# Weights loaded by casting transfers, chunk loads in 1 KB runs with the token group first, in a fused attention and feed-forward kernel

## The chip, the cores and the metric

The kernel runs on one core of a Trainium2 chip. The metric is device microseconds of one execution. Each kernel was run several times. The engines are called by their profile names: PE is the tensor engine (PEld its weight loads), DVE the vector engine, ACT the scalar engine, POOL GpSimd, and SP the engine that issues most of the transfers. Each works through its own instruction queue in the order in which the build put the instructions.

## The reference

Sliding-window causal attention (window 64) over 8 batches, 8 heads, 576 positions and head size 64 gives 4608 tokens of width 512. A feed-forward layer with squared ReLU follows.

```python
scores = q @ k.T / sqrt(64), masked to 0 <= row - column < 64, softmax
x = (softmax @ v), heads side by side          # [4608, 512]
h = np.maximum(x @ w_in, 0.0)                  # w_in  [512, 2048]
out = (h * h @ w_out).astype(np.float32)       # w_out [2048, 512]
```

Everything arrives and leaves in fp32. The kernel multiplies in fp16.

## The kernel before

The 4608 tokens are 36 chunks of 128. A chunk covers two blocks of 64 tokens, and its first block also looks at the 64 tokens before it. Four functions do a chunk's attention: T (transpose k and q on PE, evict kT on DVE and qT on ACT), S (scores on PE, exponential on ACT, mask on DVE), V (values on PE, division on DVE), and X (transpose of the result). Then come up groups (x times w_in, ReLU on ACT, square on DVE) and output matmuls (times w_out).

For V, the values lie in two forms. `v_ev` holds a chunk's own 128 tokens. `v_od` holds the 64 tokens before the chunk and its first 64. So a chunk's `v_od` is written in two halves, and the lower half comes from the chunk **before** it. The eight buffers of each form rotate:

```python
NV = 8
v_evs = [const.tile([P, H, 66], FP16, name=f"v_ev{i}") for i in range(NV)]
v_ods = [const.tile([P, H, 66], FP16, name=f"v_od{i}") for i in range(NV)]
...
nc.vector.memset(v_ods[0][0:64, :, 0:D], 0.0)

def load(i):
    ...   # three fp32 transfers on SP: k, q, v; the source is read in runs of 64 values, 256 B
    nc.gpsimd.tensor_copy(out=k16s[i][:], in_=...)          # casts to fp16 on POOL
    nc.gpsimd.tensor_copy(out=q16s[i][:], in_=...)
    v_ev, v_od, v_next = v_evs[i % NV], v_ods[i % NV], v_ods[(i + 1) % NV]
    nc.gpsimd.tensor_copy(out=v_ev[:, :, 0:D], in_=sts[2][:])
    nc.gpsimd.tensor_copy(out=v_od[64:P, :, 0:D], in_=v_ev[0:64, :, 0:D])
    if i + 1 < NCK:
        nc.gpsimd.tensor_copy(out=v_next[0:64, :, 0:D], in_=v_ev[64:P, :, 0:D])

def values(i):
    ...
    for blk in range(2):
        vv = (v_ods if blk == 0 else v_evs)[i % NV]
        nc.tensor.matmul(av[...], pms[i][...], vv[:, h, 0:65], start=True, stop=True)
```

Chunk 0 has no tokens before it. The mask sets these probabilities to zero, so what the lower half of `v_ods[0]` holds does not matter to its result, as long as it is finite.

The first eight chunks (the first stage, `NFIRST = 8`) have no earlier group to work on, so they are handled chunk by chunk with small up groups (four blocks of 128 columns at a time). After them, every group g does its up groups beside the output matmuls of group g-1 and the attention of group g+1. This is the order in which the program text of before states the first stage; `warm(n)` are filler matmuls without use to the result:

```python
load(0)
for s in load_w_in():          # 16 fp32 transfers of 256 KB, each cast (times 100) by DVE
    s()
for i in range(1, NV - 1):     # chunks 1 to 6
    load(i)
T(0), warm(6), S_(0), warm(6), V(0), warm(6), X(0), warm(4)
load(NV - 1)                   # chunk 7, AFTER V(0)
for s in load_w_out() + ffn_up_chunk(0):   # 16 more transfers, cast by POOL
    s()
T(1), S_(1), warm(2), V(1), T(2), warm(2), X(1), S_(2)
for i in range(1, NFIRST):
    up = ffn_up_chunk(i)
    up[0](), V(i + 1), T(i + 2), up[1](), up[2](), X(i + 1), S_(i + 2), up[3]()
```

And a scheduler in the build then sorts each engine's queue, by priorities and by when it thinks each instruction can start; only engines named in a "manual schedule" region keep the text's order, and what stands outside the region can still be put in between (e5 shows it).

The softmax here doesn't subtract the row's maximum and nothing guards it: scores larger than these inputs give would overflow.

## Time and profile before

| | before |
|---|---|
| time, median of 3 runs (lowest to highest) | 347.73 us (346.21 to 348.35) |
| span of the profiled execution | 345.9 us |
| PE busy over the span | 94% |
| first value matmul of chunk 0 starts at | 15.2 us |
| last matmul of the small up groups starts at | 75 us |

The busy time by window, before. Each row gives the window, its length, the busy microseconds (and instruction counts) of PE, PEld, DVE, ACT and POOL, the granted PE clock, the DMA share (packet times summed, over 16 engines; the sum can pass 1), and GB/s.

```profile
core 0: us, PE busy (x) PEld busy (x) DVE busy (x) ACT busy (x) POOL busy (x), PEclk, DMA share, GB/s
...
16.00:24.00 8.00, 5.99 (x82) 4.41 (x81) 5.49 (x15) 1.79 (x3) 0.61 (x1) 1.00 0.90 255
24.00:32.00 8.00, 4.52 (x64) 3.41 (x64) 5.46 (x14) 2.32 (x5) 5.57 (x9) 0.65 1.07 243
32.00:40.00 8.00, 7.04 (x130) 6.17 (x129) 5.76 (x14) 4.70 (x10) 6.64 (x12) 0.92 0.96 216
40.00:50.00 10.00, 8.49 (x164) 7.49 (x162) 8.56 (x19) 5.66 (x11) 9.44 (x17) 1.00 0.99 256
...
140.00:200.00 60.00, 60.00 (x532) 29.91 (x531) 40.98 (x95) 30.55 (x55) 30.57 (x50) 1.00 0.70 168
```

At 140 to 200 us PE is busy for all 60 of 60 us: nothing but less PE work could shorten that part. What a change in loads can move lies in the first 75 us, where PE has gaps, and the rows from 16 to 50 us show it working, with gaps, while transfers run at full load.

The chain of waits, before, in its first 25 us; columns are start, duration, and what.

```profile
4.12 5.49 DMA ws<-in_moe_w_in_dram
...
10.09 4.25 DMA ws<-in_moe_w_in_dram
...
14.81 3.77 DMA ws<-in_moe_w_in_dram
...
19.72 5.40 DMA ws<-in_moe_w_in_dram
```

These four transfers take 18.9 of the first 25 us, so w_in is what bounds the start.

First PE, before: start, duration, line, instruction, and in brackets how long the engine had been idle and what released it.

```profile
13.65 1.25 PE L286 MATMUL warm<-mask_inner,ident 128*128 128x512 f16 x5
15.17 0.22 PE L211 MATMUL av<-v_od_121,pm_327 128*64 128x65 f16 x1 [0.26 <-DVE pm_327 L201]
```

The first value matmul of chunk 0 starts at 15.17 us and has waited 0.26 us, for its mask. It reads `v_od_121`, which is `v_ods[0]`. Then POOL, before:

```profile
47.83 0.61 POOL L167 COPY v_od_121<-v_ev_120 64x512 f16<-64x512 f16 x1
```

At 47.83 us, chunk 7's last copy writes the same `v_od_121`, for chunk 8. It comes 33 us after the matmul, and the matmul does not wait for it, since `load(7)` stands after V(0) in the program.

### The profile page before, as it was taken

How to read it: one execution, taken by the hardware profiler on the slowest of the kernel's cores; microseconds unless marked ns; L12 is line 12 of the kernel's file. 1: busy time of each engine (PE TensorE's matmuls, PEld its weight loads, DVE VectorE, ACT ScalarE, POOL GpSimd, SP SyncE). 2: the span in 40 equal slices, each digit the busy share in tenths (PEclk: the TensorE clock that was granted, in tenths of full speed). 3: DMA queues.
4: the chain of work that ended last, by engine and by line, in shares of the span. 5: the costliest groups of instructions: out<-in, count | busy, mean ns of one | idle time of the engine just before them, and what ended most of it. 6: DMA issues, size and time to landing. Idle time of an engine off the chain costs nothing.

```text
span 345.9 us, 7917 instructions
## 1 busy us (share of the span) xinstructions
PE 324.3 (94%) x3146; PEld 178.2 (52%) x3146; DVE 207.9 (60%) x506; ACT 163.8 (47%) x289; POOL 121.5 (35%) x204
## 2 busy tenths in 40 slices
PE   1957888999999999999999999999999999999995
PEld 0346787875555555445545554455445544544442
DVE  2656988852666776676776657665675566544400
ACT  1123457544535646643664466436544654444411
POOL 4009895497753333316566544530000000000000
PEclk9996999999999999999999999999999999999998
DMA  7799987899972455546877757730011000000021
GB/s 200 249 252 239 234 247 252 207 230 228 243 172 61 93 121 123 121 124 155 212 185 182 170 135 184 185 87 27 23 45 36 30 32 32 30 30 32 35 88 62
DMA packets 122341, 46.65 MB, mean 135 GB/s; under 512 B 113600, under 2 KB 113600, under 8 KB 122304
## 3 DMA queue, kind: packets, MB, share of 16 engines
q1 hardware_dynamic: 122304, 46.15, 51.7%
q8 instruction: 24, 0.39, 0.5%
q14 instruction: 13, 0.11, 0.1%
HBM read 36.70 MB, written 9.44 MB: 133 GB/s over the span
## 4 chain that ended last, share of the span: by engine, by line
PE 83%; DVE 7%; DMA 5%; ACT 2%; SPq 1%; issue 1%; ACTq 0%
PE ops L296 37%; PE hps L250 28%; DMA ws<-in_moe_w_in_dram 5%; PE qkT_ps L173 4%; PE av L211 4%; PE xt_ps L224 2%; DVE h_397 L276 1%; DVE h_1087 L276 1%; DVE xT L226 1%; DVE w_in_sb L117 1%; PE hps_639 L271 1%; SPq L151 1%; SPq L115 0%; PE hps_1088 L271 0%; PE hps_1537 L271 0%
## 5 line engine op out<-in xcount | busy, mean ns | idle before, releaser
L250 PE MATMUL hps<-xT,w_in_sb 128*128 128x512 f16 x448 | 115.2, 379 | 0.0
L254 ACT ACTIVATE hrelu<-hps 128x512 f32<-128x512 f32 x112 | 66.8, 598 | 91.6 <-PE hps L250 90.9
L250 PEld LDWEIGHTS <-w_in_sb 128*128 128x128 f16 x448 | 43.7, 98 | 52.6 <-issue 0.3
L271 PEld LDWEIGHTS <-w_in_sb 128*128 128x128 f16 x512 | 31.2, 99 | 8.2 <-issue 3.9
L301 ACT ACTIVATE osb<-ops 128x512 f32<-128x512 f32 x36 | 21.6, 600 | 29.1 <-PE ops L296 28.9
L182 ACT ACTIVATE qT<-qkT_ps 128x512 f16<-128x512 f16 x36 | 21.5, 596 | 22.6 <-DVE kT L180 22.3
L216 DVE TENSOR_TENSOR x_sb<-av,rden 128x256 f16<-128x256 f32 x72 | 27.5, 415 | 0.1
L180 DVE COPY kT<-qkT_ps 128x512 f16<-128x512 f16 x36 | 15.2, 421 | 18.0 <-PE qkT_ps L173 17.8
L226 DVE COPY xT<-xt_ps 128x512 f16<-128x512 f16 x36 | 15.1, 420 | 12.7 <-PE xt_ps L224 12.7
L215 DVE RECIPROCAL rden<-av 128x4 f32<-128x4 f32 x72 | 11.4, 178 | 17.1 <-PE av L211 17.1
L255 DVE SCALAR_TENSOR_TENSOR h_5222<-hps,hrelu 128x512 f16<-128x512 f32 x16 | 11.1, 691 | 16.6 <-ACT hrelu L254 16.6
L296 PE MATMUL ops<-w_out_sb,h_1087 128*128 128x512 f16 x64 | 17.5, 380 | 0.0
L191 PEld LDWEIGHTS <-kT 64*128 64x128 f16 x576 | 11.0, 95 | 12.2 <-issue 9.6
L296 PE MATMUL ops<-w_out_sb,h_3120 128*128 128x512 f16 x64 | 16.5, 380 | 0.0
L296 PE MATMUL ops<-w_out_sb,h_2579 128*128 128x512 f16 x64 | 16.5, 380 | 0.0
L296 PE MATMUL ops<-w_out_sb,h_4199 128*128 128x512 f16 x64 | 16.5, 380 | 0.0
L296 PE MATMUL ops<-w_out_sb,h_3658 128*128 128x512 f16 x64 | 16.5, 380 | 0.0
L296 PE MATMUL ops<-w_out_sb,h_2041 128*128 128x512 f16 x64 | 16.5, 380 | 0.0
L296 PE MATMUL ops<-w_out_sb,h_4736 128*128 128x512 f16 x64 | 16.4, 379 | 0.0
L296 PE MATMUL ops<-w_out_sb,h_397 128*128 128x512 f16 x64 | 15.3, 380 | 0.0
L224 PE MATMUL xt_ps<-ident,x_sb 128*128 128x128 f16 x144 | 15.1, 222 | 0.1
L255 DVE SCALAR_TENSOR_TENSOR h_4736<-hps,hrelu 128x512 f16<-128x512 f32 x16 | 11.0, 689 | 6.8 <-ACT hrelu L254 6.4
(837 smaller groups left out, 611.1 us busy)
## 6 DMA issues: line engine op xcount, KB each, us to landing
out_dram<-osb SPq DMA_DIRECT2D x36, 256.0 KB, 2.2
k_st<-in_k_dram SPq DMA_DIRECT2D x32, 256.0 KB, 3.9
q_st<-in_q_dram SPq DMA_DIRECT2D x32, 256.0 KB, 4.0
v_st<-in_v_dram SPq DMA_DIRECT2D x32, 256.0 KB, 4.1
ws<-in_moe_w_in_dram SPq DMA_DIRECT2D x16, 256.0 KB, 4.2
k_st<-in_k_dram SPq DMA_DIRECT2D x8, 128.0 KB, 3.2
q_st<-in_q_dram SPq DMA_DIRECT2D x8, 128.0 KB, 3.0
v_st<-in_v_dram SPq DMA_DIRECT2D x8, 128.0 KB, 3.2
```

Source lines behind the costliest of these rows:

```text
L173: nc.tensor.transpose(out=ps[:, s, hp, :], in_=src[i][:, hp * P:(hp + 1) * P], identity=ident[:])
L180: nc.vector.tensor_copy(out=kT[:, :, 64:192], in_=ps[:, 0])
L182: nc.scalar.activation(out=qT[:], in_=ps[:, 1], func=AF.Copy, scale=1.0)
L216: nc.vector.tensor_tensor(out=x_sb[:, 4 * half:4 * half + 4, :], in0=av[:, :, 0:D], in1=rden[:].to_broadcast([P, 4, D]), op=ALU.mult)
L224: nc.tensor.transpose(out=xt[:, c, :], in_=xs[i][:, 2 * c:2 * c + 2, :], identity=ident[:])
L226: nc.vector.tensor_copy(out=xT_of(i // 4)[:, :, (i % 4) * P:(i % 4 + 1) * P], in_=xt[:])
L250: nc.tensor.matmul(hps[:], w_in_sb[:, c, f * P:(f + 1) * P], xT_of(g)[:, c, :], start=(c == 0), stop=(c == DMC - 1))
L254: nc.scalar.activation(out=hrelu[:], in_=hps[:], func=AF.Relu)
L255: nc.vector.scalar_tensor_tensor(out=h2s[g][:, f, :], in0=hps[:], scalar=0.0, in1=hrelu[:], op0=ALU.max, op1=ALU.mult)
L271: nc.tensor.matmul(hps[:, f, :], w_in_sb[:, c, (4 * fq + f) * P:(4 * fq + f + 1) * P], xT_of(g)[:, c, t0:t0 + P], start=(c == 0), stop=(c ...
L296: nc.tensor.matmul(hold["ps"][:], h2s[g][:, f, ts * P:(ts + 1) * P], w_out_sb[:, f, :], start=(f == 0), stop=(f == FFC - 1))
L301: nc.scalar.activation(out=osb[:], in_=hold["ps"][:], func=AF.Copy, scale=OUT_SCALE)
```

## The change

The intent is to take work off DVE and POOL and bytes and descriptors off the transfers, so that the first stage is shorter:

- w_in and w_out come in by eight transfers issued from POOL that cast fp32 to fp16 on the way. The 32 casts on DVE and POOL go. The scale of 100 that the w_in cast carried becomes a scale of 1e4 in the ReLU. That POOL has to issue them agrees with the Trainium skill, "DMA: Bandwidth & Descriptors", section "SWDGE vs HWDGE vs iDMA", which names GpSimd as the only engine whose transfers may cast.
- k and q of the seven first-stage chunks that lie within one batch are read in runs of 1 KB (four tokens of one head) in two transfers each. A partition then holds token group and head pair instead of a token. The token group (32 of them) is the slower dimension and the head pair (4) the faster. The rows are put right when kT and qT are evicted from PSUM, with strided reads.
- ACT casts k and q of the first stage (chunk 0's k on DVE), not POOL.
- POOL's and PE's queues in the first stage are fixed by manual-schedule regions. For this the loads of all eight chunks are written in one POOL block, ahead of the attention.

The core of the diff (cut):

```diff
-            nc.sync.dma_start(out=ws[:], in_=moe_w_in[c * P:(c + 1) * P, quar * FQ:(quar + 1) * FQ])
-            nc.vector.tensor_scalar(out=w_in_sb[:, c, ...], in0=ws[:], scalar1=W_SCALE, ...)
+        nc.gpsimd.dma_start(                     # fp32 in DRAM, fp16 in the tile
+            out=w_in_q[quar][:],
+            in_=moe_w_in[:, quar * FQ:(quar + 1) * FQ].rearrange("(c p) n -> p c n", p=P))
 ...
+                for b2 in range(2):
+                    eng.dma_start(
+                        out=st[:, b2, :],
+                        in_=rows.rearrange("(a b) (t r) d -> b t a (r d)", b=2, r=4)[b2])
 ...
+        if runs(i):
+            k_dst, q_dst = [x.rearrange("p a (i r) -> p a i r", r=4) for x in (k_dst, q_dst)]
+            k_src, q_src = [x.rearrange("p r (i a) -> p a i r", a=HP) for x in (k_src, q_src)]
+        nc.vector.tensor_copy(out=k_dst, in_=k_src)
 ...
-    load(0)
-    for s in load_w_in():
-        s()
-    for i in range(1, NV - 1):
-        load(i)
-    T(0), warm(6), S_(0), warm(6), V(0), warm(6), X(0), warm(4)
-    load(NV - 1)
-    for s in load_w_out() + ffn_up_chunk(0):
-        s()
+    with tc.manual_schedule(engines={mybir.EngineType.Pool}):
+        load(0)
+        load_w_in(0)
+        load_w_in(1)
+        cast_v(0)
+        load_w_in(2)
+        load(1)
+        load_w_in(3)
+        for i in range(2, NV):
+            load(i)
+            if i >= 6:
+                load_w_out(2 * i - 12)
+                load_w_out(2 * i - 11)
+    with tc.manual_schedule(engines={mybir.EngineType.PE}):
+        T, S_, V, X = transposes, scores, values, to_xT
+        U = up_chunk
+        T(0), warm(3), S_(0), warm(3), V(0), warm(3), X(0), warm(2)
+        U(0, 0), warm(2), U(0, 1), T(1), warm(2), S_(1), warm(2), V(1), U(0, 2), X(1), U(1, 0)
+        ...
```

## The prediction

It was made from the text, the profile of before, and the instruction order of the built changed kernel, before that kernel had run.

> **What bounds it now.** The span is 345.9 us, TensorE busy 94% (busy table). Busy time by window splits it: from about 75 to 342 us TensorE never rests (60.0 of 60 us at 140 to 200, clock 1.00), 267 us of work that the change leaves, then 4 us of drain. Only the first 75 us can move. There the chain of waits runs through w_in transfers until 25 us (5.5, 4.3, 3.8, 5.4 us), then through eight small chunk stages of about 7 us each, where DVE is busy 87 to 90% and DMA moves 210 to 255 GB/s. TensorE work in that stage is small: 32 up groups of about 0.9 us, and about 1.3 us of attention a chunk, near 39 us.
>
> **What changes by intent.** Sixteen DVE casts of w_in (0.43 us) and sixteen POOL casts of w_out (0.61 us) go; the DMA casts instead. The k and q casts of chunks 0 to 7 go to ACT (about 0.6 us each). Seven chunks' k and q load in 1 KB runs, not 256 B. Token-group-first keeps 32, not 4, as the slowest dimension on the DRAM side; the Trainium skill, "DMA: Bandwidth & Descriptors", section "Why a DMA increments its semaphore by 16 and not by 1", says that this dimension decides over how many of the 16 engines a DMA spreads. No trace here shows it yet. Strided PSUM reads may lift kT's eviction from 0.42 to about 0.6 us, hidden. Alone, all this would end the stage 10 us sooner.
>
> **What the built instruction order does** should cost more:
> 1. ACT's queue holds the k and q casts of all chunks up to 7 ahead of the first hrelu. It is in order, so no up group is squared before chunk 7's q has landed.
> 2. PE's queue holds output matmuls of group 0 among the first chunks: one that waits for the first quarter of w_out stands before chunk 1's values, the second quarter follows, the third and fourth stand before chunk 3's scores. POOL issues the first two quarters only after chunk 6's v is cast.
>
> So PE stops after chunk 1's scores until about 4.2 MB of w_in, 5.5 MB of chunks 0 to 6, 2.1 MB of w_out and part of chunk 7 have landed: 12 to 12.6 MB. At 250 to 280 GB/s (estimate from the rates above) plus 3 us of start and latency this is about 48 us (42 to 56).
>
> **Sum.** After the restart 30 up groups, most of seven chunks' attention and about 31 early output matmuls (0.22 us each) remain: 42 us of TensorE, about 47 with dependences, a colder clock and the last w_out quarters. The stage ends at about 95 us. The early matmuls take 7 us from the later 267: 95 + 260 + 4 = 359 us. Prediction: **359 us**, 8 in 10 between 347 and 373. Chances: faster by over 2% 0.06, within 2% 0.23, slower by over 2% 0.71.
>
> **What would show it.** PE almost idle from about 14 to 45 us, a lowered clock after it; the first hrelu at 35 us or later, behind ACT's casts that wait for DMA; PE's output matmuls waiting for w_out transfers; DMA over 0.8 busy until 55 us; afterwards the same full PE; kT's eviction near 0.6 us.
>
> **What would make it wrong.** DMA well above 300 GB/s would restart PE near 40 us and make it a tie. Slow casting transfers, or many us of descriptor generation on POOL (in no trace yet), would make it slower still. If PE and ACT were not held by those early instructions, with all w_in landed by 25 us, the result would be near 335 us.

## More of the kernel before

A reader of a buffer waits for the writers that stand before it in the text.

From the page of before, the lines to compare later: the kT eviction (busy us in all, mean ns of one), and the queue that carried the loads.

```profile
L180 DVE COPY kT<-qkT_ps 128x512 f16<-128x512 f16 x36 | 15.2, 421 | 18.0 <-PE qkT_ps L173 17.8
...
q1 hardware_dynamic: 122304, 46.15, 51.7%
```

## The result, and the profile after

| | before | after |
|---|---|---|
| time, median of 4 runs (lowest to highest) | 348.04 us (346.21 to 348.37) | 369.42 us (367.33 to 369.64) |
| ratio of fast runs (95% interval) | | 1.0613 (1.0572 to 1.0654) |
| profiled span | 345.9 us | 367.9 us |
| first value matmul of chunk 0 starts at | 15.2 us | 44.4 us |
| last matmul of the small up groups starts at | 75 us | 105 us |

A ratio here is the mean time of one kernel's fast runs over the mean of the other's in the same rounds, so it is not quite the ratio of the medians quoted beside it. Executions over 1.5% slower than the fastest of the same kernel are left out of the means.

The changed kernel is 6.1% slower. The busy time by window, after:

```profile
16.00:24.00 8.00, 2.00 (x19) 0.86 (x19) 0.91 (x2) 3.16 (x7) 3.69 (x6) 1.00 0.97 240
24.00:32.00 8.00, 0.00 (x0) 0.00 (x0) 0.40 (x1) 1.45 (x4) 2.66 (x5) 1.00 1.10 181
32.00:40.00 8.00, 0.00 (x0) 0.00 (x0) 0.00 (x0) 3.08 (x6) 4.59 (x8) 1.00 0.93 244
40.00:50.00 10.00, 5.59 (x43) 3.68 (x43) 1.55 (x5) 1.51 (x3) 6.75 (x11) 1.00 1.20 202
...
140.00:200.00 60.00, 60.00 (x542) 30.35 (x537) 36.72 (x86) 32.01 (x57) 21.17 (x36) 1.00 0.65 145
```

From 24 to 40 us PE does nothing at all, where before it was busy for 11.6 us. At 140 to 200 us it is as full as before. So the loss lies early on, around one long stop. PE's timeline, after, shows what it is:

```profile
21.84 0.61 PE L219 MATMUL sc<-qT,kT 64*128 64x64 f16 x16 [11.04 <-ACT qT L209]
22.39 1.46 PE L312 MATMUL warm<-mask_inner,ident 128*128 128x512 f16 x3
44.41 0.21 PE L240 MATMUL av<-v_od,pm 128*64 128x65 f16 x1 [20.57 <-POOL v_od L137]
```

PE waited twice. Before chunk 0's scores it waited 11.04 us for ACT to evict qT. Then it stood before the very first value matmul for 20.57 us, waiting for a POOL copy from line 137. That line is the copy into the **next** chunk's `v_od`. POOL's timeline, after, tells whose copy it was:

```profile
40.88 1.49 POOL L145 DMA_DIRECT2D w_out<-in_moe_w_out_dram  x2
42.41 0.61 POOL L134 CAST v_ev<-st 128x512 f16<-128x512 f32 x1
43.09 0.61 POOL L135 COPY v_od<-v_ev 64x512 f16<-64x512 f16 x1
43.75 0.61 POOL L137 COPY v_od<-v_ev 64x512 f16<-64x512 f16 x1
44.31 1.48 POOL L145 DMA_DIRECT2D w_out<-in_moe_w_out_dram  x2
```

The copy that ended at 44.36 us, just before PE went on, lies between the two pairs of w_out transfers, so by POOL's fixed order it belongs to chunk 7. With eight buffers, chunk 7's "next" buffer is `v_ods[(7 + 1) % 8]`, that is `v_ods[0]`: the one that V(0) reads. In before the same copy ran at 47.83 us and nobody waited, because it stood after V(0) in the program. In the change all eight loads stand ahead of V(0), so V(0) has to read what chunk 7's copy wrote, and waits until chunk 7's v has landed and has been cast and copied. The values in question are multiplied by masked zeros.

ACT's timeline, after, holds the other long wait, and the first ReLU:

```profile
13.42 0.62 ACT L118 CAST q<-st 128x512 f16<-128x512 f32 x1 [3.97 <-DMA st<-in_q_dram]
20.68 0.62 ACT L117 CAST k<-st 128x512 f16<-128x512 f32 x1 [6.64 <-DMA st<-in_k_dram]
21.20 0.59 ACT L209 ACTIVATE qT<-qkT_ps 128x512 f16<-128x512 f16 x1
...
40.47 0.62 ACT L118 CAST q<-st 128x512 f16<-128x512 f32 x1
49.48 0.60 ACT L279 ACTIVATE hrelu<-hps 128x512 f32<-128x512 f32 x1 [8.39 <-PE hps L302]
```

The eviction of chunk 0's qT stood in ACT's queue behind a k cast (chunk 2's, the third cast after that of chunk 0's q) that waited for its transfer until 20.68 us. The Trainium skill, "Perfetto Trace Analysis", section "Tensor Engine Instruction (MATMUL, LD_WEIGHTS)", calls ACT a strict FIFO, and this is how that looks. The last cast starts at 40.47 us, and the first ReLU only at 49.48 us. What it waited for is PE (8.39 us), not a cast.

The lines that answer to the rest of before's: the kT eviction, and the queues (the second one is that of the casting transfers).

```profile
L208 DVE COPY kT<-qkT_ps 128x512 f16<-128x512 f16 x36 | 17.1, 476 | 26.7 <-PE qkT_ps L200 26.5
...
q1 hardware_dynamic: 106880, 37.50, 44.3%
q0 software_dynamic: 4224, 4.19, 7.0%
```

The account of the span is short. Up to the end of the first stage's up groups it is 76 us before and 106 us after: 30 us lost. After that point PE is busy for 265.5 us before and 257.5 us after, with 4.4 us more in both: 8 us given back, most of it because after has already done 37 output matmuls by 106 us where before had done 8 by 76 us (143.8 us of output matmuls remain before, 137.2 after). The difference of 22 us is that of the spans.

### The profile page after: what moved, and what is told of

Read it like the earlier page. It is cut to its first block, busy times and chain, and to the rows that moved or that the text cites. A ratio compares the mean times of both kernels' runs of the same rounds, so it can differ in the third digit from the quotient of the medians.

```text
span 367.9 us, 7882 instructions
## 1 busy us (share of the span) xinstructions
PE 320.7 (87%) x3137; PEld 175.9 (48%) x3137; DVE 194.8 (53%) x464; ACT 172.4 (47%) x304; POOL 106.0 (29%) x181
## 3 DMA queue, kind: packets, MB, share of 16 engines
q1 hardware_dynamic: 106880, 37.50, 44.3%
## 4 chain that ended last, share of the span: by engine, by line
PE 81%; DMA 8%; DVE 4%; ACT 2%; SPq 2%; POOL 1%; issue 1%; ACTq 0%; POOLq 0%
PE ops L322 35%; PE hps L288 26%; PE hps L302 6%; DMA st<-in_v_dram 5%; PE av L240 4%; PE qkT_ps L200 4%; PE sc L219 3%; DMA st<-in_k_dram 2%; PE xt_ps L253 2%; DVE h L280 2%; ACT hrelu L279 1%; SPq L102 1%; DVE pm L230 1%; PE warm L312 1%; DMA st<-in_q_dram 1%
## 5 line engine op out<-in xcount | busy, mean ns | idle before, releaser
L322 PE MATMUL ops<-w_out,h 128*128 128x512 f16 x576 | 149.0, 380 | 0.1
L280 DVE SCALAR_TENSOR_TENSOR h<-hps,hrelu 128x512 f16<-128x512 f32 x144 | 99.2, 689 | 62.8 <-ACT hrelu L279 60.3
L288 PE MATMUL hps<-xT,w_in 128*128 128x512 f16 x448 | 115.0, 379 | 0.0
L322 PEld LDWEIGHTS <-h 128*128 128x128 f16 x576 | 49.5, 98 | 42.9 <-DVE h L280 0.4
L288 PEld LDWEIGHTS <-w_in 128*128 128x128 f16 x448 | 43.8, 98 | 52.9
L137 POOL COPY v_od<-v_ev 64x512 f16<-64x512 f16 x35 | 21.5, 613 | 72.0 <-PE av L240 71.3
L228 ACT ACTIVATE pm<-sc 128x512 f16<-128x512 f32 x72 | 39.2, 598 | 2.1 <-PE sc L219 1.9
L302 PE MATMUL hps<-xT,w_in 128*128 128x128 f16 x512 | 34.9, 223 | 0.3
L302 PEld LDWEIGHTS <-w_in 128*128 128x128 f16 x512 | 30.7, 100 | 4.1 <-issue 2.2
L134 POOL CAST v_ev<-st 128x512 f16<-128x512 f32 x36 | 22.1, 613 | 27.4 <-DMA st<-in_v_dram 25.6
L230 DVE TENSOR_TENSOR pm<-pm,mask_inner 128x512 f16<-128x512 f16 x56 | 24.3, 454 | 1.2 <-ACT pm L228 1.1
L219 PEld LDWEIGHTS <-kT 64*128 64x128 f16 x576 | 11.5, 95 | 25.7 <-issue 23.3
## 6 DMA issues: line engine op xcount, KB each, us to landing
w_in<-in_moe_w_in_dram POOLq DMA_DIRECT2D x4, 512.0 KB, 10.1
```

Source lines behind the costliest of these rows:

```text
L134: nc.gpsimd.tensor_copy(out=v_ev[:, :, 0:D], in_=st_v[i][:])
L219: nc.tensor.matmul(sc[hh][:, hp, blk, :], kT[r0:r0 + 64, hp, a + 64 * blk:a + 64 * blk + P], qTs[i][r0:r0 + 64, hp, 64 * blk:64 * blk + 64 ...
L228: nc.scalar.activation(out=pm[:], in_=sc[hh][:], func=AF.Exp, scale=1.0 / float(D) ** 0.5)
L230: nc.vector.tensor_tensor(out=pm[:], in0=pm[:], in1=mask, op=ALU.min)
L280: nc.vector.scalar_tensor_tensor(out=out, in0=hps, scalar=0.0, in1=hrelu, op0=ALU.max, op1=ALU.mult)
L288: nc.tensor.matmul(hps[:], w_in_q[f // 4][:, c, f % 4 * P:(f % 4 + 1) * P], xT_of(g)[:, c, :], start=(c == 0), stop=(c == DMC - 1))
```

## The experiments

The theories, as they stood after the result:

- **A, the buffer**: V(0) waits for chunk 7's copy into `v_ods[0]`, because the loads now stand ahead of V(0) and eight buffers rotate. The loss is this one dependence.
- **B, the queues** (the prediction's): ACT's casts of all chunks ahead of the first ReLU, and output matmuls that wait for w_out ahead of chunk 1's values, hold PE.
- **C, the transfers**: casting transfers or the new chunk loads are slow and deliver late.

Every experiment gave a correct result, and each was timed in three rounds beside before on the same chip. The number in brackets behind a time is before's median in those rounds. The experiments ran on four chips (e1 to e4, e5 to e8, e9 and e10, e11 and e12), so small differences between these sets are read from the ratios.

### One more buffer (e1)

```diff
-    NV = 8
+    NV = 9
...
-        for i in range(2, NV):
+        for i in range(2, NFIRST):
             load(i)
```

> The changed kernel with nine pairs of v buffers in place of eight, eight first chunks as before. Theory A (TensorE stood still from 24 to 44 us because the first value matmul reads the v_od buffer into which chunk 7's v copy goes, and the copy comes first in program order): the first value matmul moves from 44.4 us to about 24 us, and the kernel takes about 348 us (340 to 354), because the k and q casts of chunks 1 and 2 still hold ACT until about 21 us. The scheduler then also places ACT's casts and the output matmuls later by itself. Theory B (the prediction's: the order of ACT's casts and the waits for w_out are the cause by themselves): these change with it, so a gain here does not separate A from B; no gain would refute A. Theory C (casting transfers and the 1 KB loads are slow in themselves): no gain, 365 us or more.

Measured: 352.24 us [348.23], ratio 1.0113 (1.0069 to 1.0157). With nine buffers chunk 7's copy goes to the ninth, and V(0) starts at 23.2 us. From the value matmuls of e1, up to 75 us (count, shortest, median and longest in ns, first and last start in us):

```profile
L240 PE MATMUL av<-v_od,pm x56: 193/196/263, 23.2 to 71.8; 128*64 128x65 f16 x56
```

Of the loss of 21 us, 17 are gone, by one more buffer. ACT's queue had also changed with it: the first ReLU came at 28.34 us, with the casts of later chunks spread out after it. The text of the program had not been touched there. So the late casts ahead of the ReLU in after were the build's answer to a PE that would be late anyway; this reading was tested again in e12. About 4 us over before remain. The longest wait of PE that e1 still shows is the one ahead of chunk 0's scores, 10.23 us for a qT that stands behind casts in ACT's queue; whether it makes the 4 us was not separated.

### The same dependence put into before (e2)

```diff
-    T(0), warm(6), S_(0), warm(6), V(0), warm(6), X(0), warm(4)
     load(NV - 1)
+    T(0), warm(6), S_(0), warm(6), V(0), warm(6), X(0), warm(4)
```

> The kernel before with one line moved: chunk 7 is loaded (in program order) ahead of chunk 0's attention and not after it. Everything else is as before: casts on DVE and POOL, 256 B runs. Theory A: the first value matmul waits for chunk 7's v copy, near 48 us, and the kernel takes 362 to 375 us. Theories B and C, which need the change's own casts or transfers: no difference over 2% from 348 us.

Measured: 368.57 us [348.23], ratio 1.0591 (1.0543 to 1.064). From the value matmuls of e2, up to 75 us, with what their engine waited for (microseconds, times):

```profile
L211 PE MATMUL av<-v_od,pm x40: 192/197/246, 47.5 to 74.9; 128*64 128x65 f16 x40
...
its engine sat idle before it (us, times) until:
  POOL v_od L167: 31.2, 1
```

This kernel has none of the change's transfers, casts or layouts. It moves one line, and it is as slow as the changed kernel. V(0) starts at 47.5 us, after 31.2 us of waiting for the copy of line 167. So the dependence alone brings a loss of this size. Part of e2's loss came with a lower granted clock (0.50 at 40 to 50 us and 0.85 at 50 to 60 us, where after had 1.00), so the close agreement of the two totals is partly chance. Theory C is not needed for it.

### The head pair first (e3)

```diff
-                        in_=rows.rearrange("(a b) (t r) d -> b t a (r d)", b=2, r=4)[b2])
+                        in_=rows.rearrange("(a b) (t r) d -> b a t (r d)", b=2, r=4)[b2])
...
-            k_src, q_src = [x.rearrange("p r (i a) -> p a i r", a=HP) for x in (k_src, q_src)]
+            k_src, q_src = [x.rearrange("p r (a i) -> p a i r", a=HP) for x in (k_src, q_src)]
```

> The changed kernel with the partition rows ordered head pair first, token group second: the same instructions in the same order on all engines, only the DRAM side's slowest dimension is 4 and not 32. If that dimension sets how many DMA engines work on a load, each 128 KB load of seven chunks' k and q runs on 4 of 16 engines; the loads land later, chunk 7's v near 55 to 65 us, and the kernel takes 375 to 395 us. If it does not, the same as the changed kernel within 1%. kT's eviction of the plain chunks from PSUM may change from 0.69 us, as its source strides differ.

Measured: 395.13 us [348.23], ratio 1.1343 (1.1301 to 1.1385), so 25.7 us slower than after; at the upper edge of what was expected. Chunk 7's v was cast at 68.18 us, later than the expected 55 to 65. Bytes, runs and instruction order are those of after. The DRAM side's slowest dimension is 4 instead of 32. The value matmuls of e3, up to 75 us:

```profile
L240 PE MATMUL av<-v_od,pm x8: 213/244/246, 70.2 to 70.5; 128*64 128x65 f16 x8
```

And the row of its page that gives the busy tenths of the transfer engines in 40 slices of the span, with after's row below it:

```profile
DMA  3936637999999649996544630100000110001012
```

```profile
DMA  7999999899992789775265200110000000010012
```

The engines were 3 to 6 tenths busy in five of the first six slices, where after has 7 to 9, and V(0) started at 70.2 us. This fits what the prediction took from the Trainium skill, "DMA: Bandwidth & Descriptors", section "Why a DMA increments its semaphore by 16 and not by 1": the slowest dimension decides over how many of the 16 engines a transfer spreads. How many engines each transfer used was not read; the mean busy share and the time were. The order of the dimensions in the change is the good one, and it is worth 25.7 us here.

### 256 B runs instead of 1 KB (e4)

```diff
     def runs(i):
-        return i < NFIRST and len(pieces(i)) == 1
+        return False
```

> The changed kernel with k and q of all chunks loaded as before in one transfer of 256 B runs, no strided evictions. Theory A: chunk 7's v copy is still what the first value matmul waits for; loads in short runs are slightly slower, so 369 to 376 us. If the 1 KB runs are what costs, 360 us or less. kT's eviction back to 0.42 us.

Measured: 368.78 us [348.23], ratio 1.0589 (1.0541 to 1.0636): no difference to after that these rounds can tell, and 0.2 us below the expected range. The loads' queue took 47.4% of 366.9 us, 174 us, against 44.3% of 367.9 us, 163 us, in after. So the longer runs save 11 us of the engines' time, and none of it reaches the kernel. V(0) started at 45.2 us, against 44.4.

### The text's order, with V(0) ahead of chunk 7's load (e5)

The eight buffers stay. The loads are written into the first stage where they are needed, and ACT keeps the text's order as well.

```diff
-    with tc.manual_schedule(engines={mybir.EngineType.Pool}):
+    with tc.manual_schedule(engines={ET.Pool, ET.PE, ET.Activation}):
...
-        load(1)
-        load_w_in(3)
-        for i in range(2, NV):
-            load(i) ...
         T(0), warm(3), S_(0), warm(3), V(0), warm(3), X(0), warm(2)
+        L(1)                    # load(i), and w_out's quarters behind chunks 6 and 7
+        load_w_in(3)
         U(0, 0), ..., X(1), U(1, 0)
+        L(2)
         ...
         for i in range(2, NFIRST):
+            if i + 2 < NFIRST:
+                L(i + 2)
```

> The changed kernel, eight buffers, with the chunk loads interleaved in program order with the work on the first chunks, so that chunk 7's v copy comes after the first value matmul, and ACT held to program order, so that each chunk's k and q casts come just before its own transposes. The queue order of the loads and of POOL up to the w_out transfers is the same. The scheduler still puts five output matmuls, which wait for the first half of w_out (landed near 51 us in the changed kernel), ahead of chunk 3's values. Theory A: the first value matmul near 11 us, TensorE stops once more until about 51 us ahead of chunk 3's values; about 350 us (342 to 357). If those early matmuls do not matter, 340 us or less.

Measured: 358.17 us [347.65], ratio 1.0275 (1.0225 to 1.0324), 1 us beyond the expected range. V(0) now starts at 12.2 us, but PE's timeline of e5 has a new stop:

```profile
50.40 1.86 PE L322 MATMUL ops<-w_out,h 128*128 128x512 f16 x4 [12.25 <-DMA w_out<-in_moe_w_out_dram]
53.72 0.58 PE L322 MATMUL ops<-w_out,h 128*128 128x512 f16 x1 [1.46 <-DMA w_out<-in_moe_w_out_dram]
```

The build has put output matmuls of group 0 ahead of chunk 3's values, and w_out is not there. This is the fault that the prediction had named, and in after it cost nothing: after's first output matmuls ran at 53.91 us with no wait before them, since w_out had landed by then. With the first stop gone the second one takes hold.

### The same without early output matmuls (e6)

```diff
-    for g in range(1, NTB + 1):
+    with tc.manual_schedule(engines={ET.PE}):
+        group(1)
+    for g in range(2, NTB + 1):
+        group(g)
```

PE's text order now reaches through group 1, so no output matmul can move into the first stage.

> As e5, and TensorE held to program order as well for the next group, so that no output matmul comes before the up projections of the first eight chunks. Theory A: without the v dependence and without the early waits the stage goes at the pace of the arriving chunks and of about 6.5 us a chunk, ends near 67 us, and the kernel takes about 335 us (328 to 343), faster than both kernels. If the casting transfers or the 1 KB loads cost in themselves (theory C), 345 us or more.

Measured: 357.08 us [347.65], ratio 1.0242 (1.0182 to 1.0303): a miss by 14 us or more, and no better than e5. The stop for w_out is gone. What e6's value matmuls waited for, up to 75 us (microseconds, times):

```profile
its engine sat idle before it (us, times) until:
  DVE pm L230: 20.8, 27
```

And two of its windows, in the columns used above:

```profile
40.00:50.00 10.00, 7.59 (x124) 6.99 (x124) 6.31 (x15) 5.83 (x11) 6.55 (x10) 0.83 1.06 197
50.00:60.00 10.00, 7.75 (x154) 7.12 (x147) 7.25 (x18) 5.37 (x10) 1.83 (x3) 1.00 1.21 204
```

PE, its weight loads included, waited 27 times for masked probabilities before value matmuls, and it worked about three quarters of the time. A chunk's scores, exponential, mask and values follow each other too closely in the text, and the early output matmuls that had been in the way in e5 may also have filled such gaps (not measured). Undoing an order fault does not give a good order.

### The order of e6 with the dependence put back (e7)

The eight loads stand ahead of V(0) again. The k and q casts stay just ahead of their transposes, PE and ACT keep the text's order, and there are no early output matmuls. More load buffers (24 for 15) allow this.

```diff
-        T(0), warm(3), S_(0), warm(3), V(0), warm(3), X(0), warm(2)
-        L(1)
+        load(1)
         load_w_in(3)
+        for i in range(2, NV):
+            load(i) ...
+        T(0), warm(3), S_(0), warm(3), V(0), warm(3), X(0), warm(2)
...
+    def cast_kq(i, sts): ...      # called from transposes(i)
```

> The changed kernel with the v dependence kept (all eight chunks loaded ahead of the attention in program order, eight buffers), but both order faults of the prediction taken away: ACT casts k and q of a chunk just before its transposes (24 staging buffers in place of 15, so that they may wait), and no output matmul before the up projections of the first chunks. Theory A: the first value matmul still starts at 44 us, 364 to 372 us. Theory B (those two orders are the cause by themselves): 335 to 350 us.

Measured: 386.47 us [347.65], ratio 1.1099 (1.104 to 1.1157), beyond the expected range on the slow side. In this kernel neither of theory B's two faults exists, and it is still 29 us slower than e6. From 16 to 40 us PE, DVE and ACT were busy for 0.00 us:

```profile
16.00:40.00 24.00, 0.00 (x0) 0.00 (x0) 0.00 (x0) 0.00 (x0) 11.64 (x20) 1.00 1.07 231
```

PE's timeline of e7 names the wait (line 145 is the copy into the next chunk's `v_od`):

```profile
43.56 0.22 PE L250 MATMUL av<-v_od,pm 128*64 128x65 f16 x1 [30.31 <-POOL v_od L145]
```

So the dependence is enough by itself, and B is not needed. V(0) starts 30.6 us later than in e6, which is about the difference in time. That e7 is also 17 us slower than after is mostly e6's order: from V(0) to the last matmul of the small up groups, e6 takes 73.3 us and e7 73.5, but after 60.8.

### The queues of after without the dependence (e8)

Nine buffers, and the text arranged so that ACT still casts all chunks ahead of the first ReLU and the build still puts output matmuls ahead of chunk 1's values.

```diff
-    NV = 8
+    NV = 9
...
+    with tc.manual_schedule(engines={ET.Pool, ET.PE, ET.Activation}):
+        ...
+        L(2)
+        T(0), warm(3), S_(0), warm(3)
+        for i in range(3, NFIRST):
+            L(i)
+        V(0), warm(3), X(0), warm(2)
         U(0, 0), warm(2), U(0, 1), T(1), warm(2), S_(1), warm(2), V(1), ...
```

> The opposite of e7: nine v buffers, so that no value matmul waits for chunk 7, but ACT held to nearly the order of the changed kernel (the k and q casts of all eight chunks ahead of the first hrelu) and output matmuls ahead of chunk 1's values as there. If the prediction's steps can hold the stage by themselves, the first hrelu comes at about 41 us and TensorE stands before chunk 1's values until the first quarter of w_out lands, near 48 to 51 us: 358 to 368 us. If only the v dependence held it, about 352 us as with nine buffers alone.

Measured: 365.55 us [347.65], ratio 1.0514 (1.0488 to 1.0541), inside the expected range. PE's timeline of e8 shows the prediction's stop, as it was drawn:

```profile
43.05 0.61 PE L219 MATMUL sc<-qT,kT 64*128 64x64 f16 x16 [12.86 <-ACT qT L209]
...
46.85 0.58 PE L322 MATMUL ops<-w_out,h 128*128 128x512 f16 x1 [2.22 <-DMA w_out<-in_moe_w_out_dram]
```

V(0) starts near 23.7 us here, and two up groups follow (26.93 and 28.26 us). Then chunk 1's scores wait for a qT that stands behind the casts, and an output matmul for w_out. So B is enough by itself as well. In after there are two holders of the same stage that let go about 3 us apart: ACT's last cast ended at 41.1 us, chunk 7's copy at 44.4. The copy is the later one and therefore the one that binds. Taking the queues' faults away alone gained nothing (e7). Taking the copy away alone gains nearly all (e1, e12), because the queues then sort themselves anew.

### A text made for the stage (e9)

From e6: the scores of a chunk are stated one step earlier, ACT's casts come after the exponentials that PE waits for, eight pieces of the first output group are placed by hand into chunks 6 and 7, and POOL's order for the next four loads is fixed too.

```diff
         for i in range(2, NFIRST):
-            ...  S_(i + 1), U(i, 1), V(i + 1), U(i, 2), T(i + 2), X(i + 1), U(i, 3), U(i + 1, 0)
+            V(i + 1), U(i, 1), T(i + 2), U(i, 2), X(i + 1), S_(i + 2), L(i + 3), U(i, 3)
+            for _ in range(4 if i >= 6 else 0):
+                first_out.pop(0)()
+            U(i + 1, 0)
```

> An attempt at a version that beats both kernels, from e6: no v dependence (program order), each chunk's scores taken one chunk earlier, so that values do not wait for the masks behind the up groups (e6 idled up to 1.7 us there in each chunk), ACT's casts placed after the exps, eight pieces of the first output group put into the up work of chunks 6 and 7 by hand, and POOL's casts of chunks 8 to 11 in order. If the 7.8 us a chunk of e6 is a chain of waits between the engines, and not the transfers, the pace falls to about 6.2 us and the kernel takes about 342 us (332 to 350). If the transfers set the pace, 352 us or more.

Measured: 342.59 us [348.84], ratio 0.9821 (0.978 to 0.9863), at the expected number. The last matmul of the small up groups starts near 73 us, before's at 75, and the output matmuls done by then save most of the rest. The verdict at 2% is unclear, but the interval lies below 1: this kernel, with the whole change in it, beats before. No run gave before's own loads a text made in this way, so how much of the gain belongs to the change and how much to the text stays open.

### Nine buffers and 256 B runs (e10)

e1 with `runs()` returning False.

```diff
     def runs(i):
-        return i < NFIRST and len(pieces(i)) == 1
+        return False
```

> Nine v buffers as in e1, and k and q loaded in 256 B runs: do the 1 KB runs pay once nothing waits for chunk 7? In the changed kernel they took 11 us off the DMA engines' busy time and nothing off the kernel. If the transfers pace the stage once the dependence is gone, 2 to 6 us slower than e1 (354 to 358 us); if not, within 1 us of e1's 352 us, or even faster, as kT's eviction is back to 0.42 us.

Measured: 349.07 us [348.84], ratio 1.001 (0.9979 to 1.0042), the faster of the two outcomes. The comparison is not clean: the build also ordered ACT differently (qT of chunk 0 stands behind chunk 1's casts only, and V(0) starts at 20.7 us, not 23.2). It says that the change without its 1 KB runs and without the dependence equals before.

### Only the one copy moved (e12)

After with nothing changed but the place of one POOL copy in the text.

```diff
-        if i + 1 < NCK:
+        if i + 1 < NCK and i != NFIRST - 1:
             nc.gpsimd.tensor_copy(out=v_next[0:64, :, 0:D], in_=v_ev[64:P, :, 0:D])
...                                              # after the first stage's text:
+    nc.gpsimd.tensor_copy(out=v_ods[0][0:64, :, 0:D], in_=v_evs[NFIRST - 1][64:P, :, 0:D])
     for s in loads(2):
         s()
```

> The changed kernel with one POOL instruction moved: the copy of half of chunk 7's v into the first v_od buffer (for chunk 8) is written in the program after the first chunks' work, and not with chunk 7's load. Eight buffers, all else as changed. Theory A: as with nine buffers, about 352 us (350 to 355), the first value matmul near 23 us, and the scheduler's order of ACT and TensorE goes back by itself. If the ninth buffer pair helped for another reason, 365 us or more.

Measured: 353.55 us [348.65] in three fast runs (350.34 to 354.29; a fourth, of 355.79 us, counts as slow and is left out), ratio 1.0124 (1.006 to 1.0187), as expected, and like e1. The value matmuls of e12, up to 75 us:

```profile
L240 PE MATMUL av<-v_od,pm x56: 192/197/263, 23.3 to 72.8; 128*64 128x65 f16 x56
```

And the moved copy in e12's POOL timeline:

```profile
46.06 0.61 POOL L361 COPY v_od<-v_ev 64x512 f16<-64x512 f16 x1
```

The copy (line 361 here) runs at 46.06 us, even later than in after, and V(0) starts at 23.3 us, not at 44.4. Nothing about the data's arrival was improved. Only the statement order was. ACT's queue is again that of e1, with the first ReLU at 27.89 us.

### The made text with 256 B runs (e11)

e9 with `runs()` returning False, the same one-line edit as e4.

> e9, whose orders on TensorE, ACT and POOL are fixed, with 256 B runs for k and q. e10 was 3 us faster than e1, but its ACT order differed. Here it does not: if the 1 KB runs pay once nothing else holds the stage, 1 to 5 us slower than e9's 342.6 us; if the strided evictions of kT (0.69 against 0.42 us, seven times on DVE) outweigh them, up to 3 us faster.

Measured: 340.07 us [348.65], ratio 0.9746 (0.9698 to 0.9794), the fastest kernel and 2.5 us below e9 (on another chip, so by ratio 0.8% below it; the two intervals just overlap). Here PE and ACT keep their text order, so this is the cleanest test of the runs, and they show no gain. The queue of the loads took 51.4% of 339.6 us, 174.6 us, against 50.0% of 340.8 us, 170.4 us, in e9: the 1 KB runs saved 4 us of the engines' time. The kT eviction (shortest, median and longest in ns, first and last start in us) of e11:

```profile
L208 DVE COPY kT<-qkT_ps x36: 408/425/427, 6.6 to 273.8; 128x512 f16<-128x512 f16 x36
```

and of e9:

```profile
L208 DVE COPY kT<-qkT_ps x36: 409/425/692, 7.9 to 274.8; 128x512 f16<-128x512 f16 x36
```

With 256 B runs all 36 evictions take 0.41 to 0.43 us; with 1 KB runs those of the first stage take up to 0.69 us, on DVE, which is 85% busy at 50 to 60 us in e9. Chunk 0 is ready earlier as well: the first kT eviction starts at 6.6 us, not 7.9. Whether either of these two makes the 2.5 us was not separated.

## Why the prediction was right or wrong

The prediction was 359 us (347 to 373), with slower as the likely outcome. The result was 369.42 us, slower, inside the range.

**Right: where the change can act.** From 140 to 200 us PE was full in both kernels. All of the difference arose in the first stage, as the prediction said, and by the intent alone ("ends 10 us sooner", "near 335 us") the change was to be good. The versions e9 and e11, without the two stops, reached 342.59 and 340.07 us, but with a text made for the stage; with the one copy moved and nothing else, the kernel stayed at 353.55 us (e12).

**Right in size, wrong in cause: the stop.** The prediction's steps 1 and 2 said that PE's and ACT's queues hold the stage, until about 48 us (42 to 56). PE restarted at 44.4 us. That the size came out does not support the steps: both holders wait for the same last loads, and let go about 3 us apart. The first thing that held it was not in those steps: V(0) waited 20.57 us for chunk 7's copy into `v_ods[0]`, a dependence made by the order of the text and by eight rotating buffers. e2 puts that dependence into before and gets the whole loss. e7 keeps it without steps 1 and 2 and is slower still. e12 removes it alone and gets back nearly all. Steps 1 and 2 are a real second holder (e8: 365.55 us from them alone), but they also were a consequence: in e1 and e12 the build puts ACT's casts behind the first ReLU by itself. The instruction order shows which instruction stands where, not what it waits for. The prediction read a queue in which casts stood ahead of ReLUs and took that for the cause, and did not ask what the first value matmul reads and who writes it.

**Wrong point inside it: where PE stops.** It was to be "after chunk 1's scores", with 30 up groups left. PE stopped before chunk 0's values, with all 32 left. "The first hrelu at 35 us or later, behind ACT's casts": it came at 49.48 us, behind PE. ACT's casts did hold something else, chunk 0's scores, for 11.04 us; but e7, where they do not, is no faster. "PE's output matmuls waiting for w_out transfers": none waited in after; they did in e8 (2.22 us) and e5 (12.25 us).

**Mis-sized: the stage after the restart.** "42 us of TensorE, about 47 with dependences". From 44.4 to 106 us is 61.6 us, and PE was busy for 58.6 of them. Up groups alone took 34.9 us (1.09 us for each of 32, where the prediction reckoned 30 of about 0.9), 37 output matmuls 11.8 us (31 were expected to take 7), 11 warm matmuls, which the prediction had not counted, 4.8 us, and the four lines of attention 18.4 us, 2.3 us a chunk where about 1.3 was reckoned. (These line totals overlap: they add up to more than the 58.6 us.) The size could have been read from before: in its first 76 us PE is busy for 58.8 us, 8.7 of them on warm matmuls, where the prediction wrote "near 39 us". This one term is the whole difference to the result: 44.4 for 48 is 4 us less, 61.6 for 47 is 15 us more, and the remainder of 262 for 264 is 2 us less. That adds 9 us to 359, against the 367.9 us of the span.

**Right: sizes of smaller things.** kT's strided eviction was expected near 0.6 us and took 0.69 (before 0.42), hidden. This agrees in direction with the Trainium skill, "VectorE: DVE Perf Modes", section "What auto-detection actually checks", by which the faster mode open to a 16-bit read from PSUM asks for steps of one element. Transfers were to be over 0.8 busy until 55 us; the windows have 0.93 to 1.20 from 8 to 60 us. The token group as the slower dimension does spread well (e3).

**Wrong: a lowered clock after the stop.** The granted clock was 1.00 in every window of after that was read. In e2 and e8 it did fall (0.50 at 40 to 50 us in both). But in e7, whose stop is about as long as e2's, it was 1.00 from 16 to 40 us, and before had 0.65 at 24 to 32 us without such a stop. These runs give no rule for it.

**Open.** How the 4 us that e1 and e12 still lose to before divide between ACT's order and the rest was not separated; e10 gets them back with a different ACT order and different runs at once.

## What to carry to other kernels

When loads are moved ahead of compute in the program text, look at every rotating buffer: the last load of the round may write into the buffer that the first compute reads, and the first compute then waits for the last load. Here each load also writes half of the next chunk's buffer, so eight buffers were one too few for eight loads ahead. One buffer pair more, or one statement moved, was worth 16 to 17 us. When a built order looks bad, ask first whether it is a cause or the scheduler's answer to a wait it already sees: take the earliest long wait in the trace and follow its buffer back to its writer, before repairing queues.

## What the Trainium skill lacked or had wrong

- No page that was consulted says that a rotating buffer can tie the first reader to the last load of a round through program order; "Perfetto Trace Analysis", section "Identifying Dependency Chains", stops at reading semaphores. Here that dependence was worth 17 us (e1 against after) and 20 us when put into before (e2).
- "DMA: Bandwidth & Descriptors", section "Anatomy of one DMA — SWDGE (gpsimd) path", gives 2.0 us plus bytes over 436e3 for one transfer, an estimate of 4.4 us for the 1 MB read here. It does not say what casting costs or whether bytes read or written count. A casting transfer of 1 MB read and 512 KB written landed after 10.1 us (median of four, w_in) among other loads, and all eight took 7.0% of 16 engines over 367.9 us, 25.8 us, for 8.39 MB read.
- The same page, section "Why a DMA increments its semaphore by 16 and not by 1", gives the rule but not what breaking it costs a kernel: here a slowest dimension of 4 for 32 in 14 chunk loads (28 transfers) cost 25.7 us (e3).
- The same page, section "Why small descriptors are slow (HBM only)", gives a fixed cost per packet, and the saving of longer runs agrees in direction. Runs of 1 KB for 256 B saved 11 us of the engines' time in after and 4 us in e9, and the kernel gained nothing (e4) or was 0.8% slower (e9 against e11). The page does not say that putting the rows right again has its price elsewhere: 0.69 for 0.42 us on each strided eviction.
